# First rows tile by tile, halo zeroing by DMA, Silu at the end, down-projections as filling: one change to a list-scheduled spectral and MLP kernel

## The chip, the cores and the metric

The kernel runs on one core of a Trainium2 chip. The metric is device time in microseconds (us) of one execution. The kernel before takes 221.56 us (median of 3 runs, 221.0 to 221.93). Every later measurement was taken beside runs of that kernel on the same chip and in the same rounds.

A run counts as "slow" when it is more than 1.5% above the fastest run of the same kernel. Ratios and their 95% intervals use fast runs only. The record calls a difference slower or faster only when it is clear of 2%. A "profile" is one traced execution; its span is about 1.8 us shorter than the device time of the same execution.

Names used below: PE is TensorE (matmuls), DVE VectorE, ACT ScalarE, POOL GpSimd, SP SyncE. SP does no arithmetic here. It issues most DMAs, one after the other. In the profile lines PEld is TensorE's weight load, SPq an instruction with which SP issues a DMA, `psall` the PSUM buffers that matmuls write, and L812 line 812 of the kernel. KK holds the rows of k, SKB the shift rows, KAC and KTM the sums and products of the k-shift; GE is gelu of the gate and HT its product with the up-projection (the gate product).

## The reference, cut to what matters

```python
xn = layernorm(A_q)                              # 2048 x 512
# A: gated long convolution
kv = (sum of 4 shifted copies of k, each times a row of shift_k) * v
y  = irfft(rfft(kv) * rfft(ssm_k)) + kv * ssm_D  # causal convolution over 2048 rows
s  = xn * y
# B: MLP
g  = silu((gelu(xn @ w_gate) * (xn @ w_up)) @ w_down)    # 512 -> 1792 -> 512
return A_q + s * g
```

The sum of four shifted copies (the "k-shift") needs the three rows before each block of rows. For the first block these rows are zero.

## The kernel before

Each of 128 partitions holds 16 rows. The Fourier transforms are matmuls in two stages: the data (V) and the filter (HTr) go through stage 1, are stored to HBM (ZK, ZH) and read back transposed (BK, BH), and go through stage 2. The filter's spectrum is stored again (ZS) and read back as HS. VectorE multiplies the two spectra (`HB = psum * HS`), an inverse stage gives BO, which goes through HBM (ZI) to the last stage. The MLP's gate, up and down-projections (Wg, Wu, Wd) run between these stages and keep TensorE busy while transfers are under way.

The order of all instructions comes from a list scheduler in the kernel's Python code. Every operation is a task with modelled duration and a priority. `run()` simulates the engines and picks, for each, what comes next. The tasks are then emitted in that order, and **each engine runs its own instructions in that order** (in the profile after the change, the gate products stand 20.8 us behind a multiply that they do not need).

```python
class Sched:                       # cut to what the argument touches
    DMA_LAT = 2500.0               # ns: every DMA is taken to land this long after its transfer slot
    ...
    QUEUE = 1500.0
    def run(self):
        ...
        queue = 0.0                # work that already waits for ACT
        if eng == "PE":
            queue = max(free.get("ACT", 0.0) - lo, 0.0) + sum(...)
        st, t, _, en = min(mine, key=lambda c: (c[1].prio + (self.DEFER if c[1].heavy and queue > self.QUEUE else 0.0), c[0], c[1].n))
        t.start, t.eng = st, eng
        free[eng] = en
        t.end = en + self.DMA_LAT if t.nbytes else en
        ...

# input loads are tasks of engines of their own, "loadsSP" and "loadsACT"
def load(name, out_ap, in_ap, w_res, w_buf, nbytes, ring="SP"):
    ...
    return S.add([("loads" + ring, 350.0)], lambda e: dma(ring, ...), w=w_buf, prio=n_load[0], nbytes=nbytes)

def small_init():                  # the zero rows of the halo: a memset on POOL
    trk.op("POOL", lambda h: h.memset(KK[0:1, 0:3, :], 0.0), w=[R_kz])
S.add([("POOL", 1400.0)], lambda e: small_init(), w=[bKK[0]], prio=5)

def kshift(i):                     # needs the rows of KK, the halo and SKB
    op([("DVE", dur)], lambda e, h: h.tensor_tensor(KAC[...], kk(3), sk(3), ALU.mult), r=need + [bSKB], w=[a], ...)
    ...                            # three more multiplies (KTM) and adds, then times V

# reading the filter's spectrum and the data's spectrum back, 16 times
S.add([("SP", ISSUE)], ld_s, r=[bZ["S"][n]], w=[hs], prio=0.5, nbytes=524288, after=kshift_tasks)
S.add([("SP", ISSUE)], lambda e: dma(e, BK[...], z_pair(ZK, n), ...), r=bZ["K"], w=[bk], prio=-0.5, nbytes=262144)

order = S.run()
order = [t for t in order if t.eng.startswith("loads")] + [t for t in order if not t.eng.startswith("loads")]
for t in order:
    t.emit(t.eng)
```

**All input loads are emitted ahead of everything else**. An SP task that is not a load stands on SP behind every load that SP issues.

The end of the kernel before, for the last four tiles: ACT writes `tanh(p/2)`, DVE multiplies the matmul result `p` by `XN` (L1082), forms `(tanh + 1) * u` (L1084) and adds `X` (L1086), then the tile is stored.

## Time and profile before

| | before |
|---|---|
| span of the profile | 218.5 us |
| PE busy | 205.5 us (94%) |
| DVE busy | 172.6 us (79%) |
| ACT busy | 119.3 us (55%) |
| first gate matmul | 13.90 us |
| end of the last matmul to end of the span | 6.3 us |

The page of the profile, its busy times and some rows of its 40 slices. A digit is the busy share of a slice in tenths; PEclk is the granted TensorE clock in tenths.

```profile
PE 205.5 (94%) x1002; PEld 95.6 (44%) x1002; DVE 172.6 (79%) x259; ACT 119.3 (55%) x152; POOL 17.5 (8%) x42
...
PE   7599999989999999999999999899999999999980
DVE  5995998579999899998448889966899653999482
...
PEclk9699999999999999999999999999999999999997
DMA  5999999998794999977999999999993264690411
```

TensorE is the bound. It has almost no slices below 9, so the time can fall only where it starts late, waits or ends late. Here are its longest waits, from the view of who waited for whom (total us, times, longest us):

```profile
PE psall L812 <- DMA Hn<-in_A_ssm_k_dram: 2.4, 1, 2.4
PE psall L577 <- ACT BO L573: 1.4, 2, 0.8
...
PE psall L577 <- DVE HT L1050: 0.6, 1, 0.6
```

A 512-column matmul starts every 0.216 us. The Trainium skill, "TensorE: Matmul & The Clock Gate", Part 1, gives 215.7 ns start to start at full clock; this trace agrees. So within its stream TensorE has nothing to gain.

Two places in the timeline that the change is about. First the start (columns: start us, us, engine, line, operation, output<-input, count, idle time before and its releaser):

```profile
7.66 4.01 PE L812 MATMUL psall<-ident,Hn 128*128 128x128 bf16 x40 [2.39 <-DMA Hn<-in_A_ssm_k_dram]
...
9.33 2.62 DVE L764 TENSOR_SCALAR XN<-X,mv 128x512 bf16<-128x512 bf16 x4
9.47 1.37 POOL L676 MEMSET KK<- 1x1536 bf16 x1
```

The 40 filter transposes took 4.01 us because the clock was 0.5 from about 7.3 us on. Four XN operations took 2.62 us because one of them, beside the POOL memset, took 1.65 us instead of 0.40. The Trainium skill, "GPSIMD Engine Reference", specifications, says that POOL shares its SBUF interfaces with VectorE.

The k-shift and the end:

```profile
25.62 1.22 DVE L935 TENSOR_TENSOR KAC<-KK,SKB 128x2048 bf16<-128x2048 bf16 x1
```

```profile
212.75 0.42 DVE L1082 TENSOR_TENSOR XN<-psall,XN 128x256 bf16<-128x256 f32 x1
213.21 0.38 ACT L1073 ACTIVATE G<-psall 128x256 bf16<-128x256 f32 x1 [1.63 <-DVE XN L1082]
...
213.95 0.43 DVE L1084 SCALAR_TENSOR_TENSOR G<-G,XN 128x256 bf16<-128x256 bf16 x1
216.01 0.29 DVE L1086 TENSOR_TENSOR G<-G,X 128x256 bf16<-128x256 bf16 x1 [1.63 <-DMA out_dram<-G]
```

The first KAC multiply starts at 25.62 us with no wait for a DMA. At the end, the last add waits 1.63 us for a store: both halves of the last tile are one resource, so writing the second half waits until the first has been read out.

### The profile page before, as it was taken

What the parts mean: (1) busy time and instruction counts of PE and PEld (TensorE: products, weight loads), DVE (VectorE), ACT (ScalarE), POOL (GpSimd) and SP (SyncE); (2) the same over time, 40 slices, a digit from 0 to 9 for tenths busy, and PEclk for the clock granted to TensorE, in tenths of its full rate; (3) what the DMA queues carried; (4) which work ended last, traced back from release to release, by engine and by line L of the source; (5) the groups of instructions that cost most, each with busy time, mean ns of one, the idle gap of its engine ahead of it and who ended that gap; (6) DMA issues with size and microseconds to landing.
All of it is one profiled execution on the core that took longest, in us unless ns stands there. A gap on an engine that the chain in (4) does not pass through costs nothing.

```text
span 218.5 us, 2888 instructions
## 1 busy us (share of the span) xinstructions
PE 205.5 (94%) x1002; PEld 95.6 (44%) x1002; DVE 172.6 (79%) x259; ACT 119.3 (55%) x152; POOL 17.5 (8%) x42
## 2 busy tenths in 40 slices
PE   7599999989999999999999999899999999999980
PEld 2673344434444444444444444334444444444450
DVE  5995998579999899998448889966899653999482
ACT  3589887766756996867472555345343724121210
POOL 8725000012000000000100000000000000000000
PEclk9699999999999999999999999999999999999997
DMA  5999999998794999977999999999993264690411
GB/s 170 407 368 319 382 377 375 415 400 239 191 324 146 285 340 335 345 245 226 341 286 343 355 339 389 396 341 267 271 319 111 96 225 162 208 294 28 159 36 48
DMA packets 48766, 59.57 MB, mean 273 GB/s; under 512 B 13424, under 2 KB 32241, under 8 KB 48752
## 3 DMA queue, kind: packets, MB, share of 16 engines
q1 hardware_dynamic: 41376, 48.64, 69.1%
q10 hardware_dynamic: 7376, 10.75, 13.6%
q8 instruction: 8, 0.13, 0.3%
q14 instruction: 6, 0.05, 0.1%
HBM read 35.78 MB, written 20.97 MB: 260 GB/s over the span
## 4 chain that ended last, share of the span: by engine, by line
PE 61%; DMA 16%; SPq 15%; DVE 4%; ACT 2%; issue 1%; ACTq 0%
PE psall L577 61%; SPq L554 15%; DMA X<-in_A_q_dram 7%; DMA ZI<-BO 6%; DMA BH<-ZH 3%; ACT BO L573 1%; DVE stats L752 1%; DMA out_dram<-G 1%; DVE G L1084 1%; DVE XN L1082 1%; DVE XN L764 1%; DVE V L943 1%; ACT G L1073 0%; DVE G L1086 0%; DVE mv L753 0%
## 5 line engine op out<-in xcount | busy, mean ns | idle before, releaser
L577 PE MATMUL psall<-xnT,Wu 128*128 128x512 bf16 x224 | 55.5, 379 | 1.0 <-ACT BO L573 0.8
L577 PE MATMUL psall<-xnT,Wg 128*128 128x512 bf16 x224 | 53.9, 379 | 0.0
L1047 ACT ACTIVATE GE<-psall 128x512 bf16<-128x512 f32 x56 | 32.9, 597 | 37.4 <-PE psall L577 37.2
L577 PE MATMUL psall<-Wd,HT 128*128 128x512 bf16 (+1 forms) x238 | 52.3, 367 | 0.6 <-DVE HT L1050 0.6
L1050 DVE TENSOR_TENSOR HT<-psall,GE 128x512 bf16<-128x512 f32 x56 | 38.0, 687 | 16.6 <-PE psall L577 15.4
L1004 DVE TENSOR_TENSOR HB<-psall,HS 128x1024 bf16<-128x1024 f32 x32 | 37.0, 1217 | 7.1 <-PE psall L577 7.1
L577 PEld LDWEIGHTS psall<-Wd,HT 128*128 128x128 bf16 x238 | 23.1, 98 | 26.2 <-DVE HT L1050 1.3
L577 PEld LDWEIGHTS psall<-xnT,Wu 128*128 128x128 bf16 x224 | 21.6, 98 | 28.1 <-ACT BO L573 1.3
L577 PEld LDWEIGHTS psall<-xnT,Wg 128*128 128x128 bf16 x224 | 21.8, 98 | 26.2 <-ACT HTr L573 0.2
L573 ACT ACTIVATE BO<-psall 128x1024 bf16<-128x1024 f32 x16 | 16.4, 1024 | 15.4 <-PE psall L577 7.8
L1073 ACT ACTIVATE G<-psall 128x512 bf16<-128x512 f32 (+1 forms) x17 | 9.5, 576 | 20.5 <-PE psall L577 18.8
L573 ACT ACTIVATE ASH<-psall 128x1024 bf16<-128x1024 f32 x16 | 16.4, 1023 | 4.7 <-PE psall L577 4.7
L577 PE MATMUL psall<-HB,MT 128*128 128x512 bf16 x64 | 16.4, 379 | 0.0
L939 DVE TENSOR_TENSOR KTM<-KK,SKB 128x2048 bf16<-128x2048 bf16 x12 | 14.6, 1220 | 0.1
L941 DVE TENSOR_TENSOR KAC<-KAC,KTM 128x2048 bf16<-128x2048 bf16 x12 | 14.6, 1219 | 0.1
L752 DVE BATCH_NORM_STATS2 stats<-X 128x6 f32<-128x512 bf16 x16 | 10.4, 673 | 4.6 <-DMA X<-in_A_q_dram 4.6
L969 ACT ACTIVATE AST<-psall 128x1024 bf16<-128x1024 f32 x11 | 11.0, 1023 | 3.8 <-PE psall L577 3.8
L761 POOL TENSOR_TENSOR mv<-mv,NHALF 128x4 f32<-128x4 f32 (+1 forms) x5 | 5.4, 1082 | 79.8 <-DVE mv L760 79.8
L1076 DVE SCALAR_TENSOR_TENSOR G<-G,psall 128x512 bf16<-128x512 bf16 x12 | 7.9, 683 | 2.9 <-ACT G L1073 2.7
L573 ACT ACTIVATE AST<-psall 128x1024 bf16<-128x1024 f32 x9 | 9.2, 1029 | 1.6 <-PE psall L577 1.6
L577 PE MATMUL psall<-HTr,F 128*128 128x512 bf16 x32 | 9.2, 380 | 0.8 <-ACT GE L1047 0.5
L577 PEld LDWEIGHTS psall<-HB,MT 128*128 128x128 bf16 x64 | 6.2, 98 | 7.7 <-DVE HB L1004 0.4
(74 smaller groups left out, 166.8 us busy)
## 6 DMA issues: line engine op xcount, KB each, us to landing
HS<-ZS SPq DMA_DIRECT2D x16, 512.0 KB, 6.6
ZH<-ASH ACTq DMA_DIRECT2D x16, 256.0 KB, 5.6
BH<-ZH SPq DMA_DIRECT2D x16, 256.0 KB, 4.2
BK<-ZK SPq DMA_DIRECT2D x16, 256.0 KB, 4.5
ZI<-BO ACTq DMA_DIRECT2D x16, 256.0 KB, 5.2
BI<-ZI SPq DMA_DIRECT2D x16, 256.0 KB, 4.0
ZS<-AST SPq DMA_DIRECT2D x11, 256.0 KB, 4.7
ZK<-AST SPq DMA_DIRECT2D x9, 256.0 KB, 4.3
```

The costliest lines, as they stand in the source:

```text
L554: trk.dma(eng, lambda e: e.dma_start(out=out_ap, in_=in_ap), sem, r=r, w=w)
L573: return h.activation(o, i, ACTF.Copy)
L577: return h.matmul(o, lhsT=l, rhs=r, start=st, stop=sp)
L752: op([("DVE", 670.0)], lambda e, h, t=t: h.bn_stats(stats[:, t, :], X[:, t, :]), r=[bX[q][t % 4 // 2]], w=[bst[t]], rr=[R_X[t]], ww=[R_st[ ...
L939: op([("DVE", dur)], lambda e, h, j=j, m=m: h.tensor_tensor(KTM[:, m.slot, :, :], kk(j), sk(j), ALU.mult), r=need + [bSKB, a], w=[m], rr=l ...
L941: op([("DVE", dur)], lambda e, h, m=m: h.tensor_tensor(KAC[:, a.slot, :, :], KAC[:, a.slot, :, :], KTM[:, m.slot, :, :], ALU.add), r=[m], ...
L969: op([("ACT", act(1024))], lambda e, h, p=p, a=a: h.activation(ast["K"][a.slot].rearrange("p c d -> p (c d)"), ps(psl(p)), ACTF.Copy, scal ...
L1004: op([("DVE", dve(1024, 1))], lambda e, h, k=k, pk=pk, qq=qq, hs=hs: h.tensor_tensor(HB[:, qq.slot, :, :].rearrange("p c d -> p (c d)"), p ...
L1047: op([("ACT", act(512))], lambda e, h: h.activation(GE[:, g.slot, :], bank(pg), ACTF.Gelu_apprx_tanh), r=[pg], w=[g], rr=lambda: R_bank(pg ...
L1050: op([("DVE", dve(512, 1))], lambda e, h: h.tensor_tensor(HT[:, q % 2, m, :], bank(pu), GE[:, g.slot, :], ALU.mult), r=[pu, g], w=[bHT[q][m]],
L1073: op([("ACT", act(n))], lambda e, h, g=g, pc=pc: h.activation(g, pc(), ACTF.Tanh, scale=0.5), r=[p], w=[bt], rr=lambda p=p: R_bank(p), ww= ...
L1076: op([("DVE", dve(512, 1))], lambda e, h, g=g, pc=pc: h.scalar_tensor_tensor(out=g, in0=g, scalar=1.0, in1=pc(), op0=ALU.add, op1=ALU.mult ...
```

## The change

Its intent: start earlier (first rows tile by tile over both issuing engines, half of the filter next, no POOL memset, a longer warm-up so that the clock stays up), end sooner (Silu as one table function, the two halves of the last tile apart), and let down-projections run wherever VectorE is behind with urgent work. Cut to its core:

```diff
-N_WARM = 12
+N_WARM = 18
@@ the scheduler: filling now looks at ACT and DVE @@
-            queue = 0.0
+            late = {}
             if eng == "PE":
-                queue = max(free.get("ACT", 0.0) - lo, 0.0) + sum(...)
+                for e in ("ACT", "DVE"):
+                    f = free.get(e, 800.0)
+                    q = max(f - lo, 0.0) + sum(c[3] - c[0] for c in cands if c[2] == e and c[1].prio <= self.URGENT and ...)
+                    late[e] = q > self.QUEUE[e]
@@ the halo's zeros @@
-        def small_init():
-            P = lambda fn, w: trk.op("POOL", fn, w=w)
-            trk.op("POOL", lambda h: h.memset(KK[0:1, 0:3, :], 0.0), w=[R_kz])
-
-        S.add([("POOL", 1400.0)], lambda e: small_init(), w=[bKK[0]], prio=5)
+            d_kz = dsem("d_kz")
+            S.add([("SP", ISSUE)], lambda e: dma(e, KK[0:1, 0:3, :], ZERO[0:1, :].unsqueeze(1).broadcast_to([1, 3, 512]), d_kz, [R_AST["K"][0]], [R_kz]), r=[bwarm], w=[bKK[0]], prio=1, nbytes=3072)
@@ first loads @@
         load_x(0)                       # now four tiles, in turn on SP and ACT
-        load_w(0)
-        for k in range(KD):
-            load_h(k)
+        load_h(0, "SP")
+        load_h(1, "ACT")
+        load_w(0, ("SP", "ACT"))
+        load_h(2, "SP")
+        load_h(3, "ACT")
@@ gate and up are put off when DVE is late; down-projections get a lower priority @@
-            tg = S.add(..., prio=10 + q, lat=200.0)
+            tg = S.add(..., prio=10 + q, lat=200.0, heavy="DVE")
-                 w=[p], prio=9 + q - 0.5 if jt or m1 == MF else 10.05 + q, lat=200.0))
+                 w=[p], prio=9 + q + 2.2, lat=200.0))
@@ last four tiles @@
+                    op([("ACT", act(n))], lambda e, h, g=g, pc=pc: h.activation(g, pc(), ACTF.Silu), ...)
+                    op([("DVE", dve(n, 2))], lambda e, h, g=g, u=u: h.tensor_tensor(g, g, u, ALU.mult), ...)
... (tanh, L1082 and L1084 removed there; the halves of the last tile become two resources;
...  one simulated load engine for both rings; the SKB copy on POOL waits for the xnT copies;
...  one multiply of VectorE gets a lower priority;
...  the ordering of the emitted tasks stays: all loads first)
```

More of the change, by code (lines that the diff above doesn't have):

```diff
@@ L268 @@
     DMA_BW = 350.0
-    LOAD_BW = 300.0
-    QUEUE = 1500.0
+    LOAD_BW = 320.0
+    FIRST = {"loads": 900.0}
+    QUEUE = {"ACT": 1500.0, "DVE": 1500.0}
+    URGENT = 3.0
     DEFER = 9.0
@@ L274, in __init__, with add @@
         self.tasks = []
-    def add(self, opts, emit, r=(), w=(), prio=5, lat=0.0, nbytes=0, after=(), heavy=False):
+    def add(self, opts, emit, r=(), w=(), prio=5, lat=0.0, nbytes=0, after=(), heavy=None):
         t = Task()
         t.n = len(self.tasks)
-        t.opts = [(e, max(d, nbytes / (self.LOAD_BW if e == "loadsSP" else self.DMA_BW))) for e, d in opts] if nbytes else opts
+        t.opts = [(e, max(d, nbytes / (self.LOAD_BW if e == "loads" else self.DMA_BW))) for e, d in opts] if nbytes else opts
         t.r, t.w = list(r), list(w)
@@ L311, in run @@
     def run(self):
-        free = {}
+        free = dict(self.FIRST)
         ready = [t for t in self.tasks if t.nleft == 0]
@@ L319, in run @@
                 for d in t.deps:
-                    base = max(base, d.end + d.lat + (self.SEM if not d.nbytes or t.opts[0][0] != "PE" else 1000.0 if d.eng.startswith("loads") else self.HEDGE))
+                    base = max(base, d.end + d.lat + (self.SEM if not d.nbytes or t.opts[0][0] != "PE" else 1000.0 if d.eng == "loads" else self.HEDGE))
                 ok = True
@@ L330, in run @@
                     continue
-                es = [(max(base, free.get(e, 0.0)), max(base, free.get(e, 0.0)) + dur, e) for e, dur in t.opts]
+                es = [(max(base, free.get(e, 800.0)), max(base, free.get(e, 800.0)) + dur, e) for e, dur in t.opts]
                 es.sort(key=lambda x: x[1])
@@ L341, in run @@
             mine = [c for c in cands if c[2] == eng and c[0] <= lo + self.SLACK]
-            queue = 0.0
+            late = {}
             if eng == "PE":
-                queue = max(free.get("ACT", 0.0) - lo, 0.0) + sum(c[3] - c[0] for c in cands if c[2] == "ACT" and c[0] <= max(lo, free.get("ACT", 0.0)) + self.SLACK)
-            st, t, _, en = min(mine, key=lambda c: (c[1].prio + (self.DEFER if c[1].heavy and queue > self.QUEUE else 0.0), c[0], c[1].n))
+                for e in ("ACT", "DVE"):
+                    f = free.get(e, 800.0)
+                    q = max(f - lo, 0.0) + sum(c[3] - c[0] for c in cands if c[2] == e and c[1].prio <= self.URGENT and c[0] <= max(lo, f) + self.SLACK)
+                    late[e] = q > self.QUEUE[e]
+            st, t, _, en = min(mine, key=lambda c: (c[1].prio + (self.DEFER if late.get(c[1].heavy) else 0.0), c[0], c[1].n))
             t.start, t.eng = st, eng
@@ L506, in build_kernel @@
         R_G = [res(f"G{t}", G[:, t, :]) for t in range(NT)]
+        R_Gh = [res(f"Gh{i}", G[:, NT - 1, 256 * i:256 * i + 256]) for i in range(2)]
         R_HT = [[res(f"HT{j}_{m}", HT[:, j, m, :]) for m in range(MF)] for j in range(2)]
@@ L560, in load @@
             n_load[0] += 1
-            return S.add([("loads" + ring, 350.0)], lambda e: dma(ring, out_ap, in_ap, sem, [], w_res), w=w_buf, prio=n_load[0], nbytes=nbytes)
+            return S.add([("loads", 350.0)], lambda e: dma(ring, out_ap, in_ap, sem, [], w_res), w=w_buf, prio=n_load[0], nbytes=nbytes)
         def op(engs, fn, r=(), w=(), rr=(), ww=(), prio=5, lat=0.0, after=()):
@@ L580, in build_kernel @@
         B = Buf
-        bX = [[B(f"X{q}_{h}") for h in range(2)] for q in range(NQ)]
+        bX = [[B(f"X{q}_{t}") for t in range(4)] for q in range(NQ)]
         bXN = [B(f"XN{t}") for t in range(NT)]
@@ L618, in warm_up @@
                 trk.op("PE", lambda h: mm(h, bank(warm), ZERO[:, 0:128], ZERO, True, True), r=[R_AST["K"][0]], w=R_bank(warm), accum=True)
-        t_warm = S.add([("PE", N_WARM * 427.0)], warm_up, r=[bwarm], w=[warm], prio=-9)
+        t_warm = S.add([("PE", 1700.0 + N_WARM * 216.0)], warm_up, r=[bwarm], w=[warm], prio=-9)
         S.add([("POOL", 700.0)], lambda e: pool_init(), w=[bconst], prio=0)
@@ L708, in load_x, with load_w, load_h @@
             else:
-                for h in range(2):
-                    load(f"x{q}_{h}", X[:, 2 * h:2 * h + 2, :], x_dr[:, 2 * h:2 * h + 2, :], R_X[2 * h:2 * h + 2], [bX[0][h]], 262144, ("SP", "ACT")[h])
-        def load_w(i):
+                for t in range(4):
+                    load(f"x{q}_{t}", X[:, t, :], x_dr[:, t, :], R_X[t:t + 1], [bX[0][t]], 131072, ("SP", "ACT")[t % 2])
+        def load_w(i, rings=("SP", "SP")):
             f0, n = FC[i]
-            for nm, W, src in (("g", Wg, wg_dr), ("u", Wu, wu_dr)):
-                load(f"w{nm}{i}", W[:, :, 128 * f0:128 * (f0 + n)], src[:, :, 128 * f0:128 * (f0 + n)], [R_Wc[nm, i]], [bW[nm][i]], 131072 * n)
-        def load_h(k):
-            load(f"h{k}", Hn[:, k, :], h_dr[:, k, :], [R_Hn[k]], [bHn[k]], 524288, "ACT")
+            for nm, W, src, ring in (("g", Wg, wg_dr, rings[0]), ("u", Wu, wu_dr, rings[1])):
+                load(f"w{nm}{i}", W[:, :, 128 * f0:128 * (f0 + n)], src[:, :, 128 * f0:128 * (f0 + n)], [R_Wc[nm, i]], [bW[nm][i]], 131072 * n, ring)
+        def load_h(k, ring):
+            load(f"h{k}", Hn[:, k, :], h_dr[:, k, :], [R_Hn[k]], [bHn[k]], 524288, ring)
         def load_k(i):
@@ L751, in ln @@
             for t in range(4 * q, 4 * q + 4):
-                op([("DVE", 670.0)], lambda e, h, t=t: h.bn_stats(stats[:, t, :], X[:, t, :]), r=[bX[q][t % 4 // 2]], w=[bst[t]], rr=[R_X[t]], ww=[R_st[t]], prio=pr)
+                op([("DVE", 670.0)], lambda e, h, t=t: h.bn_stats(stats[:, t, :], X[:, t, :]), r=[bX[q][t % 4]], w=[bst[t]], rr=[R_X[t]], ww=[R_st[t]], prio=pr)
                 op([("DVE", 140.0)], lambda e, h, t=t: h.bn_aggr(mv[:, t, 0:2], stats[:, t, :]), r=[bst[t]], w=[bmv[q][t % 4 // 2]], rr=[R_st[t]], ww=[R_mv[t]], prio=pr)
@@ L764, in ln @@
                     op([("DVE", 420.0)], lambda e, hd, t=t: hd.tensor_scalar(XN[:, t, :], X[:, t, :], mv[:, t, 0:1], mv[:, t, 3:4], ALU.subtract, ALU.mult),
-                       r=[bX[q][t % 4 // 2], b], w=[bXN[t]], rr=[R_X[t], R_mv[t]], ww=[R_XN[t]], prio=pr)
+                       r=[bX[q][t % 4], b], w=[bXN[t]], rr=[R_X[t], R_mv[t]], ww=[R_XN[t]], prio=pr)
             return t_pw
         d_xt = dsem("d_xt")
+        xnT_tasks = []
         def xn_transpose(q):
@@ L790, in ev @@
                     return copy(e, h, xnT[:, q % 2, 2 * hf:2 * hf + 2, :, :].rearrange("p j k c -> p (j k c)"), bank16(p))
-                op([("DVE", dve(1024, 2)), ("ACT", act(1024))], ev, r=[p], w=[bxnT[q][hf]],
-                   rr=lambda p=p: R_bank(p), ww=R_xnT[q % 2][2 * hf:2 * hf + 2], prio=-1, after=af)
+                xnT_tasks.append(op([("DVE", dve(1024, 2)), ("ACT", act(1024))], ev, r=[p], w=[bxnT[q][hf]],
+                   rr=lambda p=p: R_bank(p), ww=R_xnT[q % 2][2 * hf:2 * hf + 2], prio=-1, after=af))
         d_out = []
@@ L897, in m @@
                     trk.op("PE", lambda h, c=c: mm(h, ps(s, c), F1[:, t, c, :], data, True, True), r=[R_F1[t], R_data], w=[R_ps[s][c]], accum=True)
-            s1_tasks[x].append(S.add([("PE", pe(2))], m, r=[bF1[t // 4]] + b_data, w=[p], prio=prio, lat=200.0, heavy=True))
+            s1_tasks[x].append(S.add([("PE", pe(2))], m, r=[bF1[t // 4]] + b_data, w=[p], prio=prio, lat=200.0, heavy="ACT"))
             op([("ACT", act(1024))], lambda e, h: copy(e, h, ast[x][a.slot].rearrange("p c d -> p (c d)"), ps(psl(p))),
@@ L914, in build_kernel @@
         kshift_tasks = []
-        skb = [op([("POOL", 3500.0)], lambda e, h: h.tensor_copy(SKB[:], SKR[:].rearrange("p (d j) -> p j d", j=4)), r=[bSKR], w=[bSKB], rr=[R_SKR], ww=[R_SKB], prio=3)]
+        skb = [op([("POOL", 3500.0)], lambda e, h: h.tensor_copy(SKB[:], SKR[:].rearrange("p (d j) -> p j d", j=4)), r=[bSKR], w=[bSKB], rr=[R_SKR], ww=[R_SKB], prio=3, after=xnT_tasks)]
         def kshift(i):
@@ L967, in h_stage2 @@
                   r=bZ["H"], w=[bh], prio=0.5, nbytes=262144, after=zh_tasks)
-            h2_tasks.append(S.add([("PE", pe(2))], fwd(p, BH, R_BH, bh), r=[bMT, bh], w=[p], prio=10.5, lat=200.0, heavy=True))
+            h2_tasks.append(S.add([("PE", pe(2))], fwd(p, BH, R_BH, bh), r=[bMT, bh], w=[p], prio=10.5, lat=200.0, heavy="ACT"))
             op([("ACT", act(1024))], lambda e, h, p=p, a=a: h.activation(ast["K"][a.slot].rearrange("p c d -> p (c d)"), ps(psl(p)), ACTF.Copy, scale=2.0 ** -12),
@@ L1042, in half @@
                 return f
-            tg = S.add([("PE", pe(4))], half(pg, Wg, "g"), r=[bW["g"][ci]] + bxnT[q], w=[pg], prio=10 + q, lat=200.0)
-            tu = S.add([("PE", pe(4))], half(pu, Wu, "u"), r=[bW["u"][ci]] + bxnT[q], w=[pu], prio=9 + q, lat=200.0, after=[tg])
+            tg = S.add([("PE", pe(4))], half(pg, Wg, "g"), r=[bW["g"][ci]] + bxnT[q], w=[pg], prio=10 + q, lat=200.0, heavy="DVE")
+            tu = S.add([("PE", pe(4))], half(pu, Wu, "u"), r=[bW["u"][ci]] + bxnT[q], w=[pu], prio=9 + q, lat=200.0, after=[tg], heavy="DVE")
             gu_tasks[q] += [tg, tu]
@@ L1068, in down @@
                         down_tasks[q].append(S.add([("PE", pe(m1 - m0, c1 - c0))], f, r=(bHT[q] if jt else bHT[q][m0:m1]) + bWd[m0 // 7:(m1 + 6) // 7],
-                                                   w=[p], prio=9 + q - 0.5 if jt or m1 == MF else 10.05 + q, lat=200.0))
+                                                   w=[p], prio=9 + q + 2.2, lat=200.0))
                     n = c1 - c0
-                    g, rg = G[:, t, c0:c1], [R_G[t]]
+                    g, rg = G[:, t, c0:c1], [R_G[t] if n == DM else R_Gh[c0 // n]]
                     bt = B(f"tanh{q}_{jt}")
-                    op([("ACT", act(n))], lambda e, h, g=g, pc=pc: h.activation(g, pc(), ACTF.Tanh, scale=0.5), r=[p], w=[bt],
-                       rr=lambda p=p: R_bank(p), ww=rg, prio=1, after=zh_tasks + (h2_tasks if q >= 2 else []))
                     if q < NQ - 1:
+                        op([("ACT", act(n))], lambda e, h, g=g, pc=pc: h.activation(g, pc(), ACTF.Tanh, scale=0.5), r=[p], w=[bt],
+                           rr=lambda p=p: R_bank(p), ww=rg, prio=1, after=zh_tasks + (h2_tasks if q >= 2 else []))
                         op([("DVE", dve(512, 1))], lambda e, h, g=g, pc=pc: h.scalar_tensor_tensor(out=g, in0=g, scalar=1.0, in1=pc(), op0=ALU.add, op1=ALU.mult),
@@ L1080, in down @@
                     u, x = XN[:, t, c0:c1], X[:, t, c0:c1]
-                    bu, b2 = B(f"u{t}_{c0}"), B(f"o{t}_{c0}")
-                    op([("DVE", dve(n, 1))], lambda e, h, u=u, pc=pc: h.tensor_tensor(u, pc(), u, ALU.mult), r=[p, bS[t // 2]], w=[bu],
-                       rr=lambda p=p, t=t: R_bank(p) + [R_XN[t]], ww=[R_XN[t]], prio=0.8)
-                    op([("DVE", dve(n, 1))], lambda e, h, g=g, u=u: h.scalar_tensor_tensor(out=g, in0=g, scalar=1.0, in1=u, op0=ALU.add, op1=ALU.mult),
-                       r=[bu, bt], w=[b2], rr=rg + [R_XN[t]], ww=rg, prio=1)
+                    b2 = B(f"o{t}_{c0}")
+                    op([("ACT", act(n))], lambda e, h, g=g, pc=pc: h.activation(g, pc(), ACTF.Silu), r=[p], w=[bt],
+                       rr=lambda p=p: R_bank(p), ww=rg, prio=1, after=zh_tasks + h2_tasks)
+                    op([("DVE", dve(n, 2))], lambda e, h, g=g, u=u: h.tensor_tensor(g, g, u, ALU.mult), r=[bt, bS[t // 2]], w=[b2], rr=rg + [R_XN[t]], ww=rg, prio=1)
                     op([("DVE", dve(n, 2))], lambda e, h, g=g, x=x: h.tensor_tensor(g, g, x, ALU.add), r=[b2], w=[b2], rr=rg + [R_X[t]], ww=rg, prio=1)
@@ L1125, in build_kernel @@
                 op([("DVE", dve(1024, 2))], lambda e, h, g=g, xs=xs: h.tensor_tensor(g, g, xs, ALU.mult), r=[bG[j], *bXN[ts]], w=[bGX[j]],
-                   rr=R_G[ts] + R_XN[ts], ww=R_G[ts], prio=4)
+                   rr=R_G[ts] + R_XN[ts], ww=R_G[ts], prio=6)
             else:
@@ L1129, in build_kernel @@
             R_g = R_G[ts] if j < 6 else R_XN[ts]
-            op([("DVE", dve(1024, 1))], lambda e, h, p=p, g=g: h.tensor_tensor(g, ps(psl(p)), g, ALU.mult), r=[p, *([bGX[j]] if j < 6 else [])], w=[bS[j], *([] if j < 6 else bXN[ts])],
+            op([("DVE", dve(1024, 1))], lambda e, h, p=p, g=g, f=1.0 if j < 6 else 2.0: h.scalar_tensor_tensor(out=g, in0=ps(psl(p)), scalar=f, in1=g, op0=ALU.mult, op1=ALU.mult), r=[p, *([bGX[j]] if j < 6 else [])], w=[bS[j], *([] if j < 6 else bXN[ts])],
                rr=lambda p=p, R_g=R_g: R_ps[psl(p)] + R_g, ww=R_g, prio=3)
@@ L1146, in build_kernel @@
         order = S.run()
-        order = [t for t in order if t.eng.startswith("loads")] + [t for t in order if not t.eng.startswith("loads")]
+        order = [t for t in order if t.eng == "loads"] + [t for t in order if t.eng != "loads"]
         for t in order:
```

## The prediction

> **What bounds it now.** The busy table gives TensorE 205.5 of 218.5 us (94%), VectorE 172.6, ScalarE 119.3. The timeline shows TensorE streaming almost without a break from 13.9 to 212.3 us, one 512-column matmul every 0.216 us. Its waits (who waited for whom) are small: 2.4 us for the first filter block, 1.4 for ScalarE's BO, 1.6 for others. In the windows of one microsecond the granted clock is 0.5 from 8 to 10 us, after the idle stretch that follows the warm-up. The end after the last matmul is 6.3 us. So only start, small waits and end can be won.
>
> **What the change is worth there.**
> - Start: first BN statistics at about 4.3 us instead of 5.3. Without the POOL memset (1.37 us, beside it one 0.4 us XN op took 1.65) XN is done near 10.1 instead of 11.95. First gate matmul about 11.6 instead of 13.9, but 32 filter transposes (about 1.7 us) move behind it. Longer warm-up keeps the clock: 40 transposes took 4.0 us at half clock, about 2.2 at full. Net gain about 1 us.
> - End: before, the last add waited 1.6 us for the store of the tile's other half. Silu, multiply, add and store: about 3.4 us after the last matmul. Gain 2.9 us.
> - Middle: down-projections move between the spectral blocks; the matmul total is unchanged. The waits may shrink by 1 us; DMA (share 1.04 at 120 to 160 us) can give new ones.
> Together 4 to 5 us: about 217 us, were this all.
>
> **What costs far more.** The zeroing of the halo rows KK[0:1, 0:3] becomes a 3 KB DMA on SP. The instruction order puts it behind all loads of the SP queue; the first k-shift multiply on VectorE waits for its semaphore. Before, SP could not issue its last load earlier than 34.2 to 35.1 us (SP timeline), and a 45 KB load on that queue took 11.4 us to land, like its 512 KB neighbours: small transfers wait behind large ones. The Trainium skill, "DMA: Bandwidth & Descriptors", section "Queues, rings and completion order", says that each engine consumes descriptors in ring order; the trace agrees. Estimate: 14.8 MB of loads plus about 0.8 MB of filter stores pass at the measured rates near 45 us, so the zeros land at 44 to 47. VectorE would start that multiply near 24.3 us (25.6 before); it stands about 20 us, in order, with the gate products behind it. TensorE runs on until banks and the three GE buffers are full, about 28.5 us, then stands until about 47.5. VectorE's later load waits (3.3 us) disappear, a cold clock costs up to 2 us. All on the critical path: about 19.5 us.
>
> **Prediction.** 221.6 - 4.6 + 19.5 = 236 us; range 228 to 242. Faster 5%, same 4%, slower 91%.
>
> **What would show it.** Waits of VectorE: one of about 20 us before the first KAC multiply, released by a DMA into KK; ScalarE and TensorE idle through 29 to 47 us; DMA rate in that stretch unchanged or higher. Last multiply-add-store chain 3.4 us after the last matmul. First gate matmul at 11 to 12 us; clock 1.0 in 8 to 11 us.
>
> **What would make it wrong.** The small DMA passing the queued loads, or SP issuing its loads much earlier (then about 217 us); VectorE, behind after the stall, holding TensorE up to 100 us (then 240 and more).

## The result, and the profile after

The changed kernel takes **241.4 us** (median of 4 runs, 240.6 to 242.69, all fast). The kernel before took 221.28 us in the same rounds. Ratios here and below are the mean time of one kernel's fast runs over that of the other's of the same rounds, so not quite the ratio of the quoted medians. Here it is 1.092, interval 1.085 to 1.100: slower by 9%, about 20 us.

The page of the profile after, the same rows:

```profile
PE 209.8 (88%) x1008; PEld 95.8 (40%) x1008; DVE 169.0 (71%) x254; ACT 119.9 (50%) x153; POOL 17.9 (7%) x41
...
PE   8797920099999999999999993999998999999994
DVE  8879100399988999899863624799994995459943
...
PEclk9999995559999999999999999899999999999999
DMA  6999999503349944985999999899999922929321
```

The hole is plain: TensorE is almost empty in slices 6 to 8 and VectorE in slices 5 to 7 (one slice is 6 us), and the granted clock falls to 0.5 in slices 7 to 9. A second, smaller hole is at slice 25. The first hole's cause is one line of the page's costliest groups (busy us, mean ns, then idle before it and what ended most of it):

```profile
L940 DVE TENSOR_TENSOR KAC<-KK,SKB 128x2048 bf16<-128x2048 bf16 x4 | 4.9, 1222 | 20.8 <-DMA KK<-AST 20.8
```

Read the queue that issued this DMA, SP, in the timeline:

```profile
6.50 6.12 SPq L560 DMA_DIRECT2D KK<-in_A_k_dram  x2
...
23.79 6.67 SPq L560 DMA_DIRECT2D Wd<-in_B_w_down_dram  x2
...
34.61 0.91 SPq L560 DMA_DIRECT2D X<-in_A_q_dram  x2
35.56 0.80 SPq L560 DMA_DIRECT2D KK<-AST  x1
```

SP issues 3 KB of zeros after all its loads, at 35.56 us. Many issues take 0.43 us, but the two at 23.79 us took 6.67; what held SP up there the profile does not say. Then the chain that ended last (start us, us, what):

```profile
35.56 10.20 DMA KK<-AST
45.76 0.02 issue
45.78 0.04 DVE KAC L940
...
46.93 0.69 DVE HT L1055
47.62 0.05 issue
47.67 2.74 PE psall L583 x6
```

The 3 KB took 10.2 us from issue to landing. The next lines of the timeline show who stood behind it:

```profile
45.78 1.23 DVE L940 TENSOR_TENSOR KAC<-KK,SKB 128x2048 bf16<-128x2048 bf16 x1 [20.80 <-DMA KK<-AST]
46.93 1.28 DVE L1055 TENSOR_TENSOR HT<-psall,GE 128x512 bf16<-128x512 f32 x2
...
47.67 1.46 PE L583 MATMUL psall<-xnT,Wg 128*128 128x512 bf16 x3 [16.27 <-DVE HT L1055]
47.70 0.60 ACT L1052 ACTIVATE GE<-psall 128x512 bf16<-128x512 f32 x1 [16.11 <-DVE HT L1055]
```

VectorE executes in order, so the gate products HT, which had nothing to do with the halo, stood behind the KAC multiply for 20.8 us. TensorE went on for another 6 us, until 31.4 us, when the buffers that HT would have emptied were full. Then it stood for 16.3 us and resumed at half clock: its first 8 matmuls took 3.60 us, where the same view gives 1.89 us for 8 at full clock (kernel before, at 13.90 us).

The start, to compare with before:

```profile
8.18 1.55 DVE L768 TENSOR_SCALAR XN<-X,mv 128x512 bf16<-128x512 bf16 x4
...
8.36 1.69 PE L817 MATMUL psall<-ident,Hn 128*128 128x128 bf16 x24 [1.28 <-DMA Hn<-in_A_ssm_k_dram]
```

Without the POOL memset, XN takes 1.55 us instead of 2.62. With the longer warm-up the clock is 1.0 from 8 to 12 us, so 24 transposes take 1.69 us. The first gate matmul starts at 11.87 instead of 13.90 us, but 32 of the 64 filter transposes then still have to follow.

The end:

```profile
235.66 0.38 ACT L1087 ACTIVATE G<-psall 128x256 bf16<-128x256 f32 x1 [0.16 <-PE psall L583]
...
236.07 0.29 DVE L1089 TENSOR_TENSOR G<-G,XN 128x256 bf16<-128x256 bf16 x1
...
236.40 0.29 DVE L1090 TENSOR_TENSOR G<-G,X 128x256 bf16<-128x256 bf16 x1
```

The last matmul ends at 235.62, so the end takes 3.3 us instead of 6.3. Silu needs a table of its own: one table load of 1.28 us appeared at 219.83 us, in an idle stretch of ScalarE where nobody waited for it. The Trainium skill, "ScalarE: Activation LUTs", "What ACT_TABLE_LOAD costs", gives 1283 ns for the load itself, and the trace agrees.

### The profile page after: what moved, and what is told of

Same layout as the page of the kernel before. It is cut to its first block, busy times and chain, and to the rows that moved or that the text cites. A ratio compares the mean times of both kernels' runs of the same rounds, so it can differ in the third digit from the quotient of the medians.

```text
span 238.9 us, 2904 instructions
## 1 busy us (share of the span) xinstructions
PE 209.8 (88%) x1008; PEld 95.8 (40%) x1008; DVE 169.0 (71%) x254; ACT 119.9 (50%) x153; POOL 17.9 (7%) x41
## 4 chain that ended last, share of the span: by engine, by line
PE 67%; SPq 15%; DMA 10%; ACT 3%; issue 2%; DVE 1%; ACTq 0%; DVEq 0%
PE psall L583 67%; SPq L560 15%; DMA KK<-AST 4%; DMA HS<-ZS 3%; DMA ZI<-BO 3%; ACT BO L579 1%; ACT ASH L579 1%; DVE HB L1009 1%; ACT GE L1052 0%; DVE HT L1055 0%; ACTq L560 0%; DVE G L1090 0%; DVE G L1089 0%; ACT G L1087 0%; ACT G L1079 0%
## 5 line engine op out<-in xcount | busy, mean ns | idle before, releaser
L583 PE MATMUL psall<-xnT,Wg 128*128 128x512 bf16 x224 | 55.6, 389 | 16.8 <-DVE HT L1055 16.3
L583 PE MATMUL psall<-xnT,Wu 128*128 128x512 bf16 x224 | 56.2, 384 | 0.1
L583 PE MATMUL psall<-Wd,HT 128*128 128x512 bf16 (+1 forms) x238 | 54.0, 370 | 0.0
L583 PE MATMUL psall<-HB,MT 128*128 128x512 bf16 x64 | 17.3, 395 | 4.9 <-DVE HB L1009 3.7
L579 ACT ACTIVATE ASH<-psall 128x1024 bf16<-128x1024 f32 x16 | 16.3, 1022 | 6.6 <-PE psall L583 6.6
L940 DVE TENSOR_TENSOR KAC<-KK,SKB 128x2048 bf16<-128x2048 bf16 x4 | 4.9, 1222 | 20.8 <-DMA KK<-AST 20.8
L765 POOL TENSOR_TENSOR mv<-mv,NHALF 128x4 f32<-128x4 f32 (+1 forms) x5 | 7.2, 1448 | 95.6 <-DVE mv L764 95.6
L756 DVE BATCH_NORM_STATS2 stats<-X 128x6 f32<-128x512 bf16 x16 | 10.4, 671 | 0.0
L1079 ACT ACTIVATE G<-psall 128x512 bf16<-128x512 f32 x12 | 6.8, 602 | 5.6 <-PE psall L583 5.6
```

What stands on the lines that cost most here:

```text
L579: return h.activation(o, i, ACTF.Copy)
L583: return h.matmul(o, lhsT=l, rhs=r, start=st, stop=sp)
L756: op([("DVE", 670.0)], lambda e, h, t=t: h.bn_stats(stats[:, t, :], X[:, t, :]), r=[bX[q][t % 4]], w=[bst[t]], rr=[R_X[t]], ww=[R_st[t]], ...
L765: t_pw = op([("POOL", 800.0)], lambda e, hd, ts=ts, n=n: hd.tensor_tensor(mv[:, ts, 3:4], mv[:, ts, 2:3], NHALF[:, 0:n, :], ALU.pow), r=[b ...
L1079: op([("ACT", act(n))], lambda e, h, g=g, pc=pc: h.activation(g, pc(), ACTF.Tanh, scale=0.5), r=[p], w=[bt], rr=lambda p=p: R_bank(p), ww= ...
```

## The experiments

Theory Q: the loss is the 3 KB DMA behind the loads of SP's queue; without it the change gains the 4.6 us of the prediction. Two rivals: R, the new order on the engines is itself what costs; S, a DMA into one partition is slow or disturbs other transfers, wherever it stands. There were twelve kernels, in three batches on three chips. E1 to E4 and E5, E7, E8, E10 to E12 ran 4 times each, E6 and E9 6 times.

### First batch: is it the place of one small DMA?

**E1: the changed kernel, with the zero DMA issued early.** It moves ahead of 23 of the 28 loads on SP, and is issued at 3.13 us. SP's order is the only thing that differs from the changed kernel; every other engine has the same instructions in the same order.

```diff
+KZ_AT = 10
-        order = [t for t in order if t.eng == "loads"] + [t for t in order if t.eng != "loads"]
+        loads = [t for t in order if t.eng == "loads"]
+        first = [t_zero] + loads[:KZ_AT] + t_kz + loads[KZ_AT:]
+        order = first + [t for t in order if t not in first]
```

> The changed kernel with one instruction moved: the zeroing DMA of KK stands on the SP queue behind the second filter block instead of behind all loads; no other engine's order differs. Theory Q (the zeros wait behind 14.8 MB of loads): they land at 11 to 14 us, VectorE's wait before the first KAC multiply falls from 20.8 us to under 1 us, TensorE's 16.3 us wait is gone, time 215 to 219 us. Rival R (the new order, with down-projections as filling, is itself slow): 233 us or more. If the wait for HS near 146 us (VectorE 6.4, TensorE 3.7 us) belongs to the new order and not to the stall, it is here again near 128 us and the time is nearer 219.

Measured: 224.24 us (223.28 to 226.33), ratio 1.015 (1.005 to 1.025). The KAC wait is gone; KAC starts at 24.79 us. So the stall is confirmed: one moved instruction is worth 17 us, and neither R nor S explains it. But the rest of the change is no gain of 4.6 us. It is a *loss* of about 3 us. Half of the theory falls here. The waits of TensorE, and one of VectorE, in this run name the new place:

```profile
PE psall L584 <- DVE HB L1012: 5.1, 1, 5.1
PE psall L584 <- ACT BO L580: 1.9, 2, 1.4
...
DVE HB L1012 <- DMA HS<-ZS: 7.8, 1, 7.8
```

**E2: the changed kernel, with the zeros written by a POOL memset again,** placed ahead of the SKB copy.

```diff
-            S.add([("SP", ISSUE)], lambda e: dma(e, KK[0:1, 0:3, :], ZERO[...], d_kz, ...), ...)
+            t_kz.append(S.add([("SP", ISSUE)], lambda e: trk.op("POOL", lambda h: h.memset(KK[0:1, 0:3, :], 0.0), w=[R_kz]), ...))
+        order.insert(order.index(skb[0]), t_kz[0])
```

> The changed kernel with the zeroing DMA replaced by the POOL memset of before, placed just ahead of the SKB copy on POOL; PE, VectorE and ScalarE orders as in the changed kernel. Theory Q: no stall, 215 to 219 us, within 1 us of the early DMA. Rival S (a DMA into one partition is slow or disturbs other transfers): this is clearly faster than the early DMA. Rival R: 233 or more.

Measured: 226.66 us, ratio 1.025 (1.017 to 1.032). The stall is gone here too, so not the engine that writes the zeros but the moment at which they land decided it. An early DMA does better than the memset by 2.4 us of the medians; the intervals of E1 and E2 overlap, so the size of that is not settled.

**E3: the kernel before, with nothing but its memset replaced by the DMA behind all loads.** The orders on PE, DVE and ACT are the same as before.

```diff
-            trk.op("POOL", lambda h: h.memset(KK[0:1, 0:3, :], 0.0), w=[R_kz])
+            S.add([("SP", ISSUE)], lambda e: dma(e, KK[0:1, 0:3, :], ZERO[...], d_kz, ...), r=[bwarm], w=[bKK[0]], prio=1, nbytes=3072)
```

> The kernel before with only the zeroing changed: no POOL memset, the DMA behind all loads of SP; PE, VectorE and ScalarE orders as before. Theory Q: the zeros land near 45 us, VectorE waits about 19 us, TensorE 14 to 18 us, time 236 to 242 us. Rival R: 220 to 222 us.

Measured: 238.47 us, ratio 1.079 (1.071 to 1.086), or 17.4 us. From the waits of VectorE:

```profile
DVE KAC L932 <- DMA KK<-AST: 19.9, 1, 19.9
```

The zeros were issued at 35.31 us and took 10.38 us; TensorE then waited 15.8 us. The same stall, alone, in the old kernel, costs as much as taking it away saves in the new one. Rival R is dead as far as the stall goes: here the engines have their old order.

**E4: a middle dose.** As E1, but behind the second V load.

```diff
-KZ_AT = 10
+KZ_AT = 22
```

> Dose: the zeroing DMA stands in the middle of SP's loads, behind the second V load. Theory Q: issued near 20 us, it lands near 32 us (12 us of loads ahead of it in the queue); VectorE waits 6 to 9 us; TensorE had run 6 us ahead before it stood in the changed kernel, so it waits only 0 to 3 us; time 1 to 5 us above the early DMA. If the DMA itself took 10 us wherever it stands, it would land at 30 us too, but in the early case it would then land at 13 us with nothing ahead of it but 1.6 MB; told apart by the time from issue to landing of the four cases.

Measured: 225.3 us, ratio 1.019 (1.011 to 1.027). The DMA was issued at 19.16 us and KAC started at 27.84 instead of E1's 24.79, after 3.3 us of VectorE's idle time that the profile labels "issue" (the zeros landed at 27.76 us, so it was the wait for them); TensorE waited 1.3 us for HT. The wait was smaller than expected, and the total grew by 1.1 us of the medians, within E1's interval. What follows is the order of magnitude only: a late landing costs little while TensorE's buffers carry it (some 6 us, as seen after the change) and almost its full length beyond.

The expectation also asked for the time from issue to landing in all four cases. The semaphore updates in the traces give 9.8 us (E1, landing at 12.94 us), 8.6 (E4), 10.4 (E3) and 10.2 (the changed kernel). So the place in SP's order hardly changed how long the DMA took once it was issued. What it changed is when SP came to issue it: 3.13, 19.16, 35.31 and 35.56 us.

### Second batch: why is the rest of the change no gain?

Theory F: the filling rule. Put back its priorities and the gain returns. Rival L: it is a load that arrives late in the spectral stage, the HS wait seen in E1 (the expectation of E8 calls it theory H). Rival P of the expectations: the bytes of that stage bind, whatever the order.

A piece of bookkeeping helps. The matmul work of both kernels is equal (197.9 us at the measured 0.216 and 0.054 us a step). The start of a matmul, less the work that stands before it in the order, is what TensorE has lost until then. At the first matmul on HB the kernel before had lost 12.08 us and E1 11.55; at the last one it was 14.23 and 21.49. So E1 gains 0.5 us at the start and 3.0 at the end, and loses 7.8 us more in the stage between. Sum: 4.3 us, the difference of the spans (222.8 and 218.5). The whole loss lies in the spectral stage. Most of it hangs on one wait: TensorE stood 5.1 us for HB until 131.25 us, and the granted clock was 0.5 until 136.3 us, so 5 us of work passed at half speed (about 2.5 us more, an estimate).

**E5: E1 with the old priorities of gate, up and down-projections.**

```diff
-    URGENT = 3.0
+    URGENT = 1e9
-            tg = S.add(..., prio=10 + q, lat=200.0, heavy="DVE")
+            tg = S.add(..., prio=10 + q, lat=200.0)
-                 w=[p], prio=9 + q + 2.2, lat=200.0))
+                 w=[p], prio=9 + q - 0.5 if jt or m1 == MF else 10.05 + q, lat=200.0))
... (and the priority of one VectorE multiply, from 6 back to 4)
```

> The early zeroing DMA (e1), with the priorities of the kernel before for down-projections, gate and up blocks; start and Silu end stay changed. Four HS loads now stand before the transposes for the last rows and the six BK loads, as in the kernel before. Theory F (the filling rule moved gate and up blocks ahead of the spectral stage and the HS loads behind BK, BH and ZS transfers): the wait of VectorE for HS near 121 us (7.8 us) is under 2 us, time 217 to 220 us. Rival P (the spectral stage is bound by the rate of its DMA, whatever the order): 223 to 225 us as in e1, the waits only moved.

Measured: 225.61 us, ratio 1.019 (1.012 to 1.025). No gain returns, and TensorE still waits 4.6 us for HB. Theory F falls. The chain before that wait is E1's again: an HS load that SP issued at 122.49 us, behind BK, ZS and BH loads and stores, landed 7.98 us later, and the clock was 0.5 until 137.3 us.

**E6: the kernel before, with only the new end** (Silu, halves apart).

```diff
-                    op([("ACT", act(n))], lambda e, h, g=g, pc=pc: h.activation(g, pc(), ACTF.Tanh, scale=0.5), ...)
-                    op([("DVE", dve(n, 1))], lambda e, h, u=u, pc=pc: h.tensor_tensor(u, pc(), u, ALU.mult), ...)
-                    op([("DVE", dve(n, 1))], lambda e, h, g=g, u=u: h.scalar_tensor_tensor(out=g, in0=g, scalar=1.0, in1=u, op0=ALU.add, op1=ALU.mult), ...)
+                    op([("ACT", act(n))], lambda e, h, g=g, pc=pc: h.activation(g, pc(), ACTF.Silu), ...)
+                    op([("DVE", dve(n, 2))], lambda e, h, g=g, u=u: h.tensor_tensor(g, g, u, ALU.mult), ...)
... (and the halves of the last tile as two resources, a factor of 2 in an earlier product)
```

> The kernel before with the Silu end alone: TensorE's and SP's order are those of the kernel before. Expected from the prediction's end term: 2.9 us less, 218.0 to 219.2 us; from the last matmul to the end 3.3 us instead of 6.3; a table load of 1.28 us before the first Silu that nobody waits for.

Measured: 218.22 us over six runs (215.79 to 220.04), two of them slow; ratio of the fast ones 0.983 (0.977 to 0.990). The gain at the end is real: 1.0 to 2.3% by the interval, or 2.3 to 5.0 us, which holds the 2.9 us predicted.

**E7: the kernel before, with only the filling rule.**

```diff
-    QUEUE = 1500.0
+    QUEUE = {"ACT": 1500.0, "DVE": 1500.0}
+    URGENT = 3.0
-                 w=[p], prio=9 + q - 0.5 if jt or m1 == MF else 10.05 + q, lat=200.0))
+                 w=[p], prio=9 + q + 2.2, lat=200.0))
... (with the lines of run() and the heavy= arguments of the change)
```

> The kernel before with the filling rule alone (start, zeroing and end as before). Theory F taken simply (the rule is slow by itself): 224 to 228 us. Against it: here the instruction order has six HS loads in a row behind eight BK loads and only two before them, so the wait for HS should show near 115 to 125 us with 2 to 6 us. If it shows no wait over 1 us and 220 to 222 us, the loss of e1 comes from the order that start and rule give together.

Measured: 227.94 us, ratio of two fast runs 1.023 (1.016 to 1.031); the profile fell in a slow run, so its waits (5.1 us for BO in all) are only a hint. Together with E5: the rule alone loses 5 us, and without the rule the new start loses as well. Neither part is *the* cause. Each gives the scheduler a new order, and both new orders lose; for E5 the trace puts the loss in the spectral stage, for E7 that stays a hint.

**E8: E1 with HS loads 2 to 4 directly behind the first,** from about 99 us on.

```diff
+        for n in (1, 2, 3):
+            order.remove(hs_loads[n])
+            order.insert(order.index(hs_loads[n - 1]) + 1, hs_loads[n])
```

> e1 with three instructions of SP moved: the second to fourth HS loads stand directly behind the first (near 99 us) instead of behind the transposes, BK, ZS and BH; every other engine's order is that of e1. Theory H (the loss of e1 against the kernel before sits in these HS loads being issued at 120 us or later): VectorE's 7.8 us and TensorE's 5.1 us waits near 121 to 131 us are gone, time 217 to 220 us. Rival P (bound by the DMA rate): the waits come back later in the stage, time 222 to 225 us.

Measured: 222.83 us, ratio 1.008 (1.003 to 1.014). The wait for HS is gone, and part of its time went into a new wait, in the timeline of TensorE:

```profile
112.82 1.01 PE L584 MATMUL psall<-BH,MT 128*128 128x512 bf16 x2 [3.14 <-DMA BH<-ZH]
```

Three loads of 512 KB had been put ahead of a BH load that was needed first. Rival L is right in kind: it is the order of the loads. But "earlier" is not the answer for every load when the queue is full.

### Third batch: bytes or order?

From 100 to 160 us the DMA engines are busy at a share near 1 (1.03 before, 0.93 in E1 with its hole). So one may blame the amount of traffic, or the order in which it passes. In E1 the queue of SP around the loads in question reads (the last line is from the chain of waits):

```profile
99.49 0.45 SPq L561 DMA_DIRECT2D HS<-ZS  x1
...
105.24 4.16 SPq L783 DMA_TRANSPOSE xnT<-XN  x1
109.52 3.06 SPq L561 DMA_DIRECT2D BK<-ZK  x6
...
118.19 1.49 SPq L561 DMA_DIRECT2D BH<-ZH  x3
119.73 1.34 SPq L561 DMA_DIRECT2D HS<-ZS  x2
...
119.73 9.09 DMA HS<-ZS
```

The second HS load is issued at 119.73 us and lands 9.09 us later. The kernel before had issued its first four at 99.76 to 104.72 us, ahead of the transposes and the BK loads.

**E9: old order, with the parts that do not disturb it:** E6, plus the early zero DMA in place of the memset, plus 18 warm-up matmuls.

```diff
-            for i in range(N_WARM):
+            for i in range(N_WARM + 6):
-        S.add([("POOL", 1400.0)], lambda e: small_init(), w=[bKK[0]], prio=5)
+            t_kz.append(S.add([("SP", ISSUE)], lambda e: dma(e, KK[0:1, 0:3, :], ZERO[...], d_kz, ...), ...))
+        first = [t_zero] + loads[:at] + t_kz + loads[at:]
```

> The kernel before with the Silu end, the zeroing as an early DMA (no POOL memset) and 18 warm-up matmuls; all other orders as in the kernel before. From e6: 218.2 us; the memset gone lets XN end about 1 us earlier, the longer warm-up saves up to 1.8 us of half clock, but the first transposes also wait for the filter loads, so 216.5 to 218.5 us. Slower than e6 by over 1 us would speak against the early DMA.

Measured: 217.46 us over six runs, one of them slow; ratio of the fast ones 0.984 (0.980 to 0.989). It beats the kernel before by 1.6%, and cannot be told from E6.

**E10: E1 with every HS load cut to half its bytes,** and **E11: the same in the kernel before,** as a control. The second half of each product uses the first half's filter values, so they compute something else. (The comparison with the reference passed nevertheless, within its tolerance.)

```diff
-                src = bass.AP(ZS, n * 192 * 2 * DM, [[2 * DM, 128], [128 * DM, 2], [1, 2 * DM]])
+                src = bass.AP(ZS, n * 192 * 2 * DM, [[2 * DM, 128], [1, 2 * DM]])
-                    ... HS[:, hs.slot, k, :, :] ...
+                    ... HS[:, hs.slot, 0, :, :] ...
```

> Wrong result on purpose: e1 with each HS load cut to its first half (256 KB instead of 512 KB), 4.2 MB less in the spectral stage; both HB products read that half; all instruction orders as in e1. Theory P (the loss of e1 is waiting for DMA in a stage whose queues are full): VectorE's 7.8 us wait for HS falls under 2 us, TensorE's waits in 100 to 180 us fall from 7 us to under 3, time 216 to 219 us. Rival O (the order itself costs, through buffers or priorities on the engines): 222 us or more.

> Control, wrong result on purpose: the same cut in the kernel before. Theory P: its small waits for BO and BH in the stage (1.6 us) fall, 219.5 to 221 us; so e10 ends 2 to 4 us below this control (start and end gains), where e1 was 3 us above the kernel before. Rival O: e10 stays 2 us or more above this control.

Measured: E10 218.47 us, ratio of three fast runs 0.987 (0.982 to 0.992); E11 218.17 us, ratio 0.989 (0.984 to 0.994). Halving these bytes gains 1.1% in the old order and 2.8% in E1's, so E1 was indeed hurt more by traffic. But E10 came out level with its control, not below it as expected, and its profile fell in its one slow run, which still shows a wait of 4.3 us for HB and so says nothing of the fast ones. Fewer bytes help. This pair alone does not say that bytes are the cause.

**E12: E1 with HS loads 2 to 4 moved between the first BK loads,** behind the transposes. Only SP's order differs from E1; all bytes stay.

```diff
+        for n, m in ((1, 1), (2, 2), (3, 3)):
+            order.remove(hs_loads[n])
+            order.insert(order.index(bk_loads[m]) + 1, hs_loads[n])
```

> e1 with the second to fourth HS loads moved between the first BK loads (behind the transposes for the last rows), not ahead of BH and ZS as in e8; all other engines as in e1. If the loss is only a bad order of the SP queue: the waits for HS near 121 us and for BH near 112 us (3.1 us in e8) are both under 1 us, time 217.5 to 220 us. If the bytes of the stage bind: 221 to 224 us, with waits later in the stage, as in e8.

Measured: **218.17 us** (217.87 to 218.77, all fast), ratio 0.988 (0.983 to 0.993). Its queue:

```profile
104.90 3.92 SPq L783 DMA_TRANSPOSE xnT<-XN  x1
108.95 1.01 SPq L561 DMA_DIRECT2D BK<-ZK  x2
110.00 0.47 SPq L561 DMA_DIRECT2D HS<-ZS  x1
...
112.05 0.75 SPq L561 DMA_DIRECT2D HS<-ZS  x1
```

The longest wait of TensorE in this stage:

```profile
PE psall L584 <- ACT BO L580: 1.4, 2, 1.2
```

The waits for HS and for BH are both gone from TensorE's list; the longest left in this stage is 1.2 us, for BO. With the waits the half clock went too: the four runs of E12 were granted a mean clock of 0.998 to 1.000, those of E1 0.982 to 0.990. Three moved instructions are worth 6 us (ratio 1.015 to 0.988, each beside the kernel before on its own chip), as much as halving 16 loads, with not a byte less. So the loss of the spectral stage in E1 was the order of SP's queue. E12 contains the whole change, with four SP instructions in other places, and is 1.2% faster than the kernel before. That is 1.6 to 3.8 us by the interval: the 4 to 5 us of the prediction are not reached even without the stall and the late HS loads.

## Why the prediction was right or wrong

Slower was right, and 241.4 us lies within 228 to 242, near its upper edge. The centre of 236 was low: the middle cost 5 to 7 us where a gain of 1 was forecast. That the total still fell inside the range, by 0.6 us, was luck in part.

| term | predicted us | measured us | from |
|---|---|---|---|
| stall behind the queue | +19.5 | +17 to +19 | E3 (17.4), the change against E1 (17.2 of medians); 19.1 by the bookkeeping up to the first matmul on HB |
| start | -1 | -0.5 | bookkeeping, E1 |
| end | -2.9 | -3.0 | 6.3 to 3.3 us after the last matmul; E6 agrees |
| middle | -1 | +5 to +7 | +4.8 in the changed kernel by the bookkeeping; without the stall (E1) +7.8, or 6.9 from its ratio (+3.4 us) less start and end |
| sum | +14.9 | about +20 | ratio 1.092 |

- **The stall: right in mechanism, place and size.** Landing was predicted at 44 to 47 us and came at 45.76. VectorE's wait was predicted near 20 us and was 20.8. The queueing was predicted from a 45 KB load that took 11.4 us; the 3 KB took 10.2. The prediction cited the Trainium skill, "DMA: Bandwidth & Descriptors", "Queues, rings and completion order": a ring's descriptors are consumed in order. The trace agrees. TensorE ran on to 31.4 us, not 28.5, so it waited 16.3 us and not 19; then it worked at half clock until 52.7 us, about 2.5 us more (an estimate), where the prediction allowed up to 2. Up to the first matmul on HB the changed kernel had lost 19.1 us more than E1. But it lost 3 us less than E1 in the spectral stage, so taking the stall away gains only 17 us: the terms of the sum do not simply add.
- **The start: right in its steps, about half in size** (0.5 us of 1). First gate matmul 11.87 us (predicted 11.6), clock 1.0 from 8 to 12 us. XN was done at 9.7 us instead of the predicted 10.1.
- **The end: right** to within 0.1 us (3.0 us gained, 2.9 predicted).
- **The step that failed is "The waits may shrink by 1 us" and with it "Together 4 to 5 us: about 217 us, were this all".** Without the stall the change takes 224.2 us (E1), not 217. The prediction added in the same sentence that DMA "can give new ones", but gave this no number. What happened there is a second case of the very mechanism it had found in the first 45 us: loads behind others on SP. The order "HS late, behind xnT, BK and BH" stood in the changed kernel's instruction order before any run; the prediction checked the queue position of one DMA, not of those that the spectral stage waits for.

Why does the scheduler produce such orders? What its code shows: it takes every DMA to land 2.5 us after its transfer slot, and it keeps the zero DMA on an engine "SP" that is separate from "loads", although SP issues both, one after the other. What the traces show: 10.2 us for the zeros, and 6.7 us (median) to 10.5 us (longest) for the HS loads of E1. That the wrong model leads to the bad orders is argued, not shown: no run changed the model. What is shown (E1, E12) is that moving four instructions on one queue takes the change from 1.092 to 0.988.

Left open: which waits cost E7 its time in its fast runs; how long the 3 KB would take with nothing else under way; how large the benefit of an early DMA over the memset is; and whether E12's new start can be combined with E9's gains. E6, E9 and E12 cannot be told apart by these runs.

## What to carry to other kernels

A small DMA waits first for its turn on the engine that issues it (here until 3.13 or 35.56 us) and then, beside busy traffic, takes about as long as its large neighbours (here 8.6 to 10.4 us for 3 KB). So for everything that an in-order engine waits for, look up where its DMA stands on the issuing engine, and not how many bytes it has. When a change reorders work in a stage whose DMA engines are busy all the time, check that queue for every load which the bound engine depends on: three loads moved between others were worth as much as halving sixteen. And test a change of several parts by undoing the suspected part alone: here it confirmed the expected loss, and showed that the expected gain was not there either.

## What the Trainium skill lacked or had wrong

- "DMA: Bandwidth & Descriptors", "Anatomy of one DMA": it gives a fixed 2.0 us plus bytes at 436 GB/s, fitted on the GpSimd path. For these DMAs on SP it would estimate 2.0 us for 3 KB and 3.2 us for 512 KB; the runs show 8.6 to 10.4 us for the 3 KB in its four places, and 6.7 us median, 10.5 us longest, for the 512 KB HS loads. The first 128 KB tile of X, with nothing ahead of it on SP, landed 2.8 us after its issue in the changed kernel, near the 2.3 us that the fit would estimate. A sentence is missing that the fit does not hold for a DMA behind others.
- The same page, "Issuing engines are not separate DMA queues": it calls the time to initiate a DMA usually small against the DMA itself. Here many issues took 0.43 us, but two together took 6.12 us and two others 6.67 us, and SP was busy issuing loads until 35.5 us. I found no page that says how much may be outstanding before the issuing engine is held up.
- "TensorE: Matmul & The Clock Gate", Part 1: it says that the clock goes cold after at least one idle window of about 3.4 us, free-running. The window length fits: in the profile after, the clock fell at about 35.7 us and rose at about 52.7 us, which is 5.0 windows (estimates from the mean clock of single microseconds). But in the kernel before it fell at about 7.3 us, only 2.0 us after the warm-up's last matmul at 5.26 us. By that window length the window that ended then held 1.4 us of matmuls (an estimate), so a window needn't be wholly idle.
- "ScalarE: Activation LUTs", table sets: the page lists no set for Silu. The trace shows one more table load, 1.28 us, between the last gelu and the first Silu, which the kernel before, with tanh in that place, did not have.
